# Scores of sixteen later units made in the first seven steps and kept in DRAM; ten early units transposed on TensorE

## The chip, the cores and the metric

The kernel runs on one NeuronCore of a Trainium2 chip. The metric is device time in microseconds (us) for one execution. The kernel before takes 1468.56 us, the median of three runs (1467.57 to 1470.6). One more execution was taken with the hardware profiler; it took 1466.93 us, and its traced span is 1465.2 us.

## What is computed

```python
scores = scale * np.matmul(q, k.transpose(0, 1, 3, 2))       # 8 batches x 8 heads, 576 x 576, head dim 64
kth = np.partition(scores, -32, axis=-1)[..., -32:-31]       # the 32nd largest of each row
scores = np.where(scores >= kth, scores, -1000000000.0)
scores = scores - np.max(scores, axis=-1, keepdims=True)
attn = np.exp(scores)
attn = attn / (np.sum(attn, axis=-1, keepdims=True) + 1e-09)
x = np.matmul(attn, v)                                       # brought to 4608 tokens x 512
h = x @ w_in                                                 # 512 -> 2048
out = np.maximum(0.01 * h, h) @ w_out                        # 2048 -> 512
```

All inputs are float32 except that the weights come as 64-bit words, which the kernel rounds to float32 itself in a prologue.

## The kernel before, in words

**Units and steps.** The attention is cut into 144 units. A unit is 128 query rows of one pair of heads (or twice 64 rows, of the rows left over by 576 = 4 x 128 + 64), so its scores are a tile `s_sb` of 128 partitions x 2 x 576. A batch has 18 units. The main loop (L540) goes over steps s = 0 to 147; four units are in work at once:

- `top_k` of unit s on VectorE (L244): a max and a min of the two halves (L251), then four rounds of MAX8 and MATCH_REPLACE8 (L256, L259). `slot()` puts out one round at a time between the other work of the step.
- `mask` of unit s-1 on GpSimd (L267 to L270), and its exponentials and sums on ScalarE (L273, L278).
- of unit s-2 ("older"): the reciprocals on VectorE (L282), the normalising on ScalarE (L285), then the transposing of the weights into a tile `wT`. The usual way, `transpose` (L287), is by DMA: ScalarE copies the tile in two halves of 16-bit words (`split`, L294), each is written to DRAM (L295), and a transposing DMA reads them back (L299). The other way, `transpose_in_haste` and `keep_transposed` (L301, L312), is nine TensorE transposes into two PSUM tiles and two ScalarE copies (L315). It is used for the units of the tuple `HASTY`, which is (14, 15, 23, 31).
- `scores` (L203): at the end of every even step TensorE makes the scores of units s+2 and s+3 into two "wide" and one "narrow" PSUM tiles (L220), and ScalarE copies them into two `s_sb` tiles (L227), of which there are five.
- `weigh_values` (L329, matmuls L336): the values of two units, at the place that `values_at` (L450) names, and `keep_values` (L350), which copies them on ScalarE into `x`. Normally these copies come late in the step. `at_once` (L562) brings them right after the matmuls, where a chunk of tokens gets complete, and two steps after a unit of `HURRIED` (15, 23, 31).

**The MLP.** When all values of a chunk of tokens (128 for the first two, 256 afterwards) are kept, its MLP becomes ready (`mlp`, L380: first product L360 or L392, activation by ScalarE L365 or L398, second product L404, output copy L413). `mlp_steps` puts out pieces of it between the other operations of each step, as many as a budget allows, which is worked out from the backlog and the step in which the next chunk gets ready (`slot_budget`, L475).

**What sets the order.** The whole block stands under a manual schedule: the order in which the program calls the operations is the order in each engine's queue. [...]So TensorE, ScalarE, GpSimd and VectorE are bound to each other by the sequence of calls within a step, and only the buffers (five `s_sb`, three `wT`, two wide and one narrow PSUM tile, two `ml` tiles for the MLP) let one run ahead of another. All DMAs are issued by SP.

**The start.** Before step 0 the weights are loaded in 16 pieces through three `raw` buffers and rounded on all engines; the first two units' scores are made there (`first_scores`, L229). `load_more` (L489) loads later queries, keys and values; the queries and keys of pairs 5, 6 and 7 of each eight are put into `raw` buffers.

For steps below 20 (`HURRY`), except one and two steps after a hurried unit, the flag `late` puts the reciprocals and normalising of `older` after the second slot of the step.

Of the kernel before, what the change touches and what calls it, by code (L numbers as in the profile page):

```python
# [9 lines left out]
F32 = mybir.dt.float32  # L10
U32 = mybir.dt.uint32
U16 = mybir.dt.uint16
# [8 lines left out]
def kernel(  # L21
# [13 lines left out]
    nc = tc.nc  # L35
    NPAIR, P, S = qT.shape
    D = P // 2
# [9 lines left out]
    HS = S // 2  # L47
# [3 lines left out]
    WCH = 1024  # L51
# [5 lines left out]
    LOADED, LOADED_V = 5, 5  # L57
# [4 lines left out]
    raws = ctx.enter_context(tc.tile_pool(name="raws", bufs=3))  # L62
    work = ctx.enter_context(tc.tile_pool(name="work", bufs=2))
    small = ctx.enter_context(tc.tile_pool(name="small", bufs=5))
    halves = ctx.enter_context(tc.tile_pool(name="halves", bufs=3, space=bass.MemoryType.DRAM))
    ps_sc = ctx.enter_context(tc.tile_pool(name="ps_sc", bufs=1, space=bass.MemoryType.PSUM))
    ps_ml = ctx.enter_context(tc.tile_pool(name="ps_ml", bufs=2, space=bass.MemoryType.PSUM))

# [13 lines left out]
    gT = const.tile([P, NFC, CHMAX], F32, name="gT")  # L82
# [7 lines left out]
    def piece(n):  # L90

        if n < NPIECE // 2:
            j, c = divmod(n, HP)
            return w_in[c][:, j * WCH:(j + 1) * WCH]
        f = 2 * (n - NPIECE // 2)
        return w_out[f // 4][:, f % 4:f % 4 + 2, :].rearrange("p g n -> p (g n)")
# [3 lines left out]
    def load_weights(n):  # L100
        if n >= NPIECE:
            return
        if not AS_WORDS:
            nc.sync.dma_start(piece(n), weights[n])
            return
        raw_of[n] = raws.tile([P, WCH, 4], U16, name="raw")
        flat = raw_of[n].rearrange("p n w -> p (n w)")
        for m, c0, c1 in ROUNDED:
            if m == n:
                nc.sync.dma_start(flat[:, 4 * c0:4 * c1], weights[n][:, 4 * c0:4 * c1])  # L110
# [48 lines left out]
    qk_of, v_of = {}, {}  # L159
# [69 lines left out]
    def first_scores(u):  # L229

        ps = [ps_sc.tile([P, 2, 512], F32, name="wide", bufs=2) for i in range(2)]
        for half in range(2):
            for i, pi, side, r0 in u.parts:
                qt, kt = qk_of[pi]
                d = slice(side * D, (side + 1) * D)
                nc.tensor.matmul(ps[i][:, half, 0:HS], qt[d, u.q0:u.q0 + P],
                                 kt[d, half * HS:(half + 1) * HS], start=True, stop=True)
        yield
        u.both = work.tile([P, 2, S], F32, name="s_sb", bufs=5)
        u.s = [u.both[:, i, :] for i in range(2)]  # L240
        for i in range(2):
            nc.scalar.copy(u.s[i].rearrange("p (h n) -> p h n", h=2), ps[i][:, :, 0:HS])

    def top_k(u):  # L244

# [180 lines left out]
    def mlp_steps(budget):  # L426
        owed[0] += budget
        while owed[0] > 0:
            if running[0] is None:
                if not ready:  # L430
                    owed[0] = 0.0
                    return
                running[0] = mlp(ready.pop(0))
            cost = next(running[0], None)
            if cost is None:
                running[0] = None
            else:
                owed[0] -= cost
                backlog[0] -= cost
# [3 lines left out]
    LAG = 3  # L443
    HURRY = 20
    HURRIED = (15, 23, 31)
    HASTY = (14, 15, 23, 31)
    UNHURRIED = 14
    MIDDLE, END = 0, 1

# [4 lines left out]
        return (n | 1) + LAG - ((n | 1) in HURRIED), END  # L454

    steps = units

    def unit(n):
        return steps[n] if 0 <= n < len(steps) else None

    done_tokens, ready_at = [0] * len(CHUNKS), []
    for n, u in enumerate(steps):
        ch, _ = x_at(u.b * S + u.q0)
# [11 lines left out]
    def slot_budget(s):  # L475

        after = [at for (at, _), _ in ready_at if at >= s]
        until = after[0] if after else s
        if len(after) >= len(CHUNKS) - EARLY:
            return EARLY_SHARE  # L480
        return backlog[0] / ((until + 1 - s) * SLOTS)
# [4 lines left out]
    with tc.manual_schedule():  # L486
        last = {p: n for n, u in enumerate(steps) for p in u.pairs}

        def load_more(s):  # L489

            for of, load, n, lag in ((v_of, load_v, LOADED_V, LAG + 1), (qk_of, load_qk, LOADED + 3, 8)):
                while len(of) < NPAIR and (len(of) < n or last[len(of) - n] + lag <= s):
                    load(len(of))
                    if lag > LAG + 1 and len(of) > n:
                        break


        for n in range(3):
            load_weights(n)
        jobs = [round_weights(*job) for job in ROUNDED] if AS_WORDS else [iter(())] * len(ROUNDED)  # L500
        for n in range(len(jobs) + 1):
            if n == len(jobs) - 1:
                first = first_scores(steps[0])
                next(first, None)
            for job in jobs[max(n - 1, 0):n + 1][::-1]:
                next(job, None)
            if n == len(jobs) - 1:
                next(first, None)
                load_v(0)
                load_v(1)  # L510
            elif n == len(jobs):
                for _ in first_scores(steps[1]):
                    pass
            if n:
                load_weights(n + 2)
            if 0 <= n - len(jobs) + HP + 1 < HP:
                load_qk(n - len(jobs) + HP + 1)

        def weights_of(u):
            reciprocals(u)  # L520
            normalize(u, 0)
            normalize(u, 1)

        def values(*place):
            due = [u for n, u in enumerate(steps) if values_at(n) == place]
            if due:
                po = ps_sc.tile([P, 2, 512], F32, name="wide", bufs=2)[:, 0, 0:2 * P]
                po = po.rearrange("p (u n) -> p u n", u=2)
            else:
                return ()  # L530
            for n, u in enumerate(due):
                weigh_values(u, po[:, n, :])
            return [(u, po[:, n, :]) for n, u in enumerate(due)]

        def keep(weighed, *place):
            for u, po in weighed:
                keep_values(u, po)
            attended(*place)

        for s in range(len(steps) + LAG + 1):  # L540
            cur, old, older, new = unit(s), unit(s - 1), unit(s - 2), ()
            if s % 2 == 0:
                new = [u for u in steps[s + 2:s + 4] if u]
            picks = top_k(cur) if cur else iter(())
            budget = slot_budget(s)

            def slot():
                next(picks, None)

            at_first = s < HURRY and s - 2 in HURRIED  # L550
            if at_first:
                weights_of(older)
            slot()
            if old:
                mask(old, 0)
                mask(old, 1)
            late = s < HURRY and not {s - 1, s - 2} & set(HURRIED)
            if older and not late and not at_first:
                weights_of(older)
            mlp_steps(budget)  # L560
            weighed = values(s, MIDDLE)
            at_once = s - 2 in HURRIED or any(at == (s, MIDDLE) for at, _ in ready_at)  # L562
            if at_once:
                keep(weighed, s, MIDDLE)
            slot()
            if older and late:
                weights_of(older)
            if s - 2 in HASTY:
                transpose_in_haste(older)
            mlp_steps(budget)  # L570
            if old:
                exponents(old, 0)
            mlp_steps(budget)
            if older:
                keep_transposed(older) if s - 2 in HASTY else transpose(older, lambda: mlp_steps(budget))
            if not older or s - 2 in HASTY:
                mlp_steps(budget)
            slot()
            slot()
            mlp_steps(budget)  # L580
            if old:
                exponents(old, 1)
                sums(old)
            mlp_steps(budget)
            if not at_once:
                keep(weighed, s, MIDDLE)
            if new and s < HURRY:
                scores(new)
            keep(values(s, END), s, END)
            if new and s >= HURRY:  # L590
                scores(new)
            budget = slot_budget(s + 1)
            mlp_steps(budget)
            load_more(s)
        mlp_steps(1e9)

# [57 lines left out]
```

## Time and profile before

| what | value |
|---|---|
| median of three runs | 1468.56 us |
| the profiled execution | 1466.93 us, span 1465.2 us |
| TensorE (PE) busy | 1395.2 us, 95% of the span |
| VectorE (DVE) busy | 1320.3 us, 90% |
| ScalarE (ACT) busy | 1100.4 us, 75% |
| GpSimd (POOL) busy | 1097.0 us, 75% |
| DMA | 222.30 MB, 152 GB/s on the mean |
| PE in the chain that ended last | 81% of the span; DVE 16% |
| step 0 begins, VectorE's last instruction ends | 60.9 us, some 1380 us |

A page of the profile gives, for one execution, the busy time of each engine; the span in 40 equal slices, with a digit for the busy share (9 is 90% or more); the granted clock of TensorE in the same slices; groups of instructions by line, as `line engine op out<-in partitions x elements xcount | busy us, mean ns of one | idle before, and what ended it`. A table of stages gives, for a stretch of the span, the busy time (and number of instructions) of each engine, then the granted clock, the DMA share and GB/s. A timeline gives start, length, engine, line, and in square brackets the idle time of that engine before the instruction, and which other one ended it. PEld is TensorE's weight load. One float32 matmul of the program is two MATMUL rows in a trace; a transpose is one.

### The profile page before, as it was taken

To read this page: it belongs to the slowest core of one execution; us is meant where nothing else is said; L and a number is where in the kernel's file an instruction comes from. 1 tells how busy PE (TensorE), PEld (TensorE's weight loads), DVE (VectorE), ACT (ScalarE), POOL (GpSimd) and SP (SyncE) were. 2 spreads that over 40 slices of the span, in tenths; PEclk is the share of its full clock that TensorE was granted. 3 is DMA by queue.
4 is the path that set the end of the run, shared out by engine and by line. 5 is a ranking of instruction groups with operands and counts; after the bars stand their busy time and mean duration, and the time that the engine had idled before them with its cause. 6 is when DMAs were issued, how large, how long until landed. Compare 5 with 4: busy or idle time off the path is not lost.

```text
span 1465.2 us, 24106 instructions
## 1 busy us (share of the span) xinstructions
PE 1395.2 (95%) x8066; PEld 927.8 (63%) x8068; DVE 1320.3 (90%) x3401; ACT 1100.4 (75%) x1984; POOL 1097.0 (75%) x744
## 2 busy tenths in 40 slices
PE   7617999999999999999999999999999999999999
PEld 2314548575757676767676767666666666666674
DVE  7999999999999999999999999999999999999600
ACT  8658878777887777777777777777777777777710
POOL 3388888878888888787878888878788878787700
PEclk9957999999999999999999999999999999999999
DMA  9834534654366455665567545655467555664510
GB/s 329 304 85 133 146 105 116 171 154 136 107 196 185 129 137 155 171 185 137 146 168 193 141 138 132 194 174 148 128 167 202 136 140 144 155 141 132 148 45 14
DMA packets 388940, 222.30 MB, mean 152 GB/s; under 512 B 333904, under 2 KB 333904, under 8 KB 386896
## 3 DMA queue, kind: packets, MB, share of 16 engines
q1 hardware_dynamic: 388816, 220.77, 53.7%
q8 instruction: 63, 1.03, 0.3%
q14 instruction: 61, 0.50, 0.1%
HBM read 46.14 MB, written 92.01 MB: 94 GB/s over the span
## 4 chain that ended last, share of the span: by engine, by line
PE 81%; DVE 16%; ACT 1%; issue 1%; DMA 0%; POOL 0%; DVEq 0%; SPq 0%; ACTq 0%; POOLq 0%
PE pz L404 31%; PE ph L392 30%; PE wide L336 10%; DVE tops L256 6%; PE wide L220 6%; DVE pairs L259 5%; PE narrow L220 3%; DVE pairs L251 2%; DVE w_out L155 1%; DVE scale L152 1%; DVE w_in L155 1%; DMA raw<-in_weights_dram 0%; DVE top L133 0%; DVE scale L131 0%; ACT s_sb L285 0%
## 5 line engine op out<-in xcount | busy, mean ns | idle before, releaser
L269 POOL TENSOR_SCALAR pen<-s_sb,tops 128x576 f32<-128x576 f32 x288 | 637.7, 2214 | 208.7 <-DVE tops L256 144.5
L256 DVE MAX8 tops<-pairs 128x8 f32<-128x288 f32 (+1 forms) x1152 | 635.9, 591 | 0.0
L404 PE MATMUL pz<-w_out,gT 128*128 128x512 f32 x1152 | 505.1, 595 | 2.4 <-ACT scale L365 2.4
L392 PE MATMUL ph<-x,w_in 128*128 128x256 f32 x2176 | 482.9, 381 | 0.9 <-ACT gT L398 0.9
L259 DVE MATCH_REPLACE8 pairs<-tops,pairs 128x288 f32<-128x288 f32 (+1 forms) x864 | 460.2, 538 | 0.0
L392 PEld LDWEIGHTS ph<-x,w_in 128*128 128x128 f32 x2176 | 409.4, 190 | 77.7 <-issue 22.2
L270 POOL TENSOR_TENSOR s_sb<-s_sb,pen 128x576 f32<-128x576 f32 x288 | 406.6, 1412 | 24.0
L404 PEld LDWEIGHTS pz<-w_out,gT 128*128 128x128 f32 x1152 | 216.4, 190 | 267.2 <-issue 262.5
L294 ACT COPY split<-s_sb 128x1152 uint16<-128x1152 uint16 x280 | 309.4, 1146 | 0.0
L285 ACT ACTIVATE s_sb<-s_sb,rz 128x576 f32<-128x576 f32 x288 | 207.6, 773 | 43.4 <-DVE rz L282 43.4
L273 ACT ACTIVATE s_sb<-s_sb,nbias 128x576 f32<-128x576 f32 x288 | 222.3, 772 | 12.8 <-POOL s_sb L270 12.8
L251 DVE TENSOR_TENSOR pairs<-s_sb 128x576 f32<-128x576 f32 x288 | 213.5, 780 | 9.9
L336 PEld LDWEIGHTS wide<-wT,vt 128*64 128x64 f32 x3200 | 161.7, 139 | 65.1 <-issue 34.6
L336 PE MATMUL wide<-wT,vt 128*64 128x128 f32 (+1 forms) x3200 | 179.1, 268 | 22.4 <-ACT s_sb L227 21.1
L398 ACT ACTIVATE gT<-ph 128x512 f32<-128x512 f32 x136 | 80.7, 593 | 56.3 <-PE ph L392 55.6
L227 ACT COPY s_sb<-wide 128x704 f32<-128x704 f32 x142 | 107.2, 755 | 21.0 <-PE wide L220 21.0
L350 ACT COPY x<-wide 128x128 f32<-128x128 f32 (+1 forms) x160 | 32.2, 260 | 112.5 <-PE wide L336 112.4
L220 PE MATMUL wide<-kt,qt 64*128 64x352 f32 (+1 forms) x392 | 76.4, 503 | 26.0 <-ACT s_sb L227 23.0
L413 ACT COPY o_sb<-pz 128x512 f32<-128x512 f32 x36 | 21.1, 586 | 98.0 <-PE pz L404 98.0
L227 ACT COPY s_sb<-narrow 128x448 f32<-128x448 f32 x142 | 68.7, 537 | 1.2 <-PE narrow L220 0.6
L282 DVE RECIPROCAL rz<-ze 128x2 f32<-128x2 f32 x144 | 22.3, 155 | 45.9 <-ACT ze L278 45.8
L259 DVE MATCH_VALUE_LOAD pairs<-tops,pairs 128x8 f32 x864 | 62.6, 72 | 0.0
(61 smaller groups left out, 623.2 us busy)
## 6 DMA issues: line engine op xcount, KB each, us to landing
apart<-split SPq DMA_DIRECT2D x280, 288.0 KB, 2.1
raw<-in_weights_dram SPq DMA_DIRECT2D x15, 1024.0 KB, 6.7
vt<-in_vk_dram SPq DMA_DIRECT2D x32, 320.0 KB, 3.4
out_dram<-o_sb SPq DMA_DIRECT2D x36, 256.0 KB, 2.6
qt<-in_qT_dram SPq DMA_DIRECT2D x20, 288.0 KB, 3.2
kt<-in_kT_dram SPq DMA_DIRECT2D x20, 288.0 KB, 3.7
raw<-in_qT_dram SPq DMA_DIRECT2D x12, 288.0 KB, 3.2
raw<-in_kT_dram SPq DMA_DIRECT2D x12, 288.0 KB, 3.6
```

Of the source, the lines that this page charges most:

```text
L220: nc.tensor.matmul(to[r0:r0 + u.rows, i, :], qt[d, u.q0:u.q0 + u.rows], kt[d, k0:k1], start=True, stop=True)
L251: nc.vector.tensor_tensor(pairs[:, :, n, :], u.both[:, :, 0:HS], u.both[:, :, HS:S], op)
L256: nc.vector.max(out=u.tops[:, i, r, :], in_=rest[i])
L259: nc.vector.match_replace(out=rest[i], in_to_replace=u.tops[:, i, r, :], in_values=rest[i], imm_value=LOWEST)
L269: nc.gpsimd.tensor_scalar(pen, u.s[i], u.tops[:, i, ROUNDS - 1, 7:8], MASKED, ALU.is_lt, ALU.mult)
L270: nc.gpsimd.tensor_tensor(u.s[i], u.s[i], pen, ALU.add)
L273: nc.scalar.activation(u.s[i], u.s[i], AF.Exp, bias=u.nbias[:, i:i + 1], scale=SCALE, accum_out=u.z[:, i:i + 1])
L285: nc.scalar.activation(u.s[i], u.s[i], AF.Copy, bias=0.0, scale=u.rz[:, i:i + 1])
L294: nc.scalar.copy(split, pairs[:, :, h])
L336: nc.tensor.matmul(po[side * D:(side + 1) * D, o, :], vt[:, c, side, :], u.wT[:, c + side * NKC if c + 1 < NKC else c, r:r + n], start=(c ...
L392: nc.tensor.matmul(ph[:, i, 0:n], w_in[c][:, f * P:(f + 1) * P], x[c][:, 0:n], start=(c == 0), stop=(c == HP - 1),)
L404: nc.tensor.matmul(pz[0:m, 0:DMODEL], gT[:, f, r0:r0 + m], w_out[f // 4][:, f % 4, :], start=(f == 0), stop=(f == NFC - 1),)
```

## The change

Three things are changed together.

1. The scores of 16 units, in four sets {24, 25, 32, 33}, {40, 41, 48, 49}, {56, 57, 64, 65} and {72, 73, 80, 81}, are made at the ends of steps 0 to 6 (4, 2, 2, 3, 1, 3 and 1 units). For each set `load_early` loads two keys tiles and four query slices into a `raw` buffer; three sets in the prologue, the fourth when the first has been used. `keep_scores` makes a unit's scores with four matmuls of 288 columns into two PSUM tiles, copies them on ScalarE into one of three slots of `gT` (free until the first MLP), and writes them to a DRAM tile. `fetch_scores` reads them back into an `s_sb` tile, one unit a step, in the step three before that of the unit, after the transposing of `older`. The `scores` calls of steps 22, 30, 38, 46, 54, 62, 70 and 78 fall away.
2. Units 0 to 9 join `HASTY`: they are transposed on TensorE, in steps 2 to 11. And `at_once` now asks for `HASTY` instead of `HURRIED`, so that the values of steps 5 and 9 are copied right after their matmuls too (those of steps 7 and 11 were already).
3. While scores are still to be kept, `load_more` loads the queries and keys of no more than five pairs, so that the `raw` buffers stay free; pairs 5, 6 and 7 follow after step 6.

```diff
+    def load_early(us):
+        raw = raws.tile([P, WCH, 4], U16, name="raw").rearrange("p n w -> p (n w)").bitcast(F32)
+        at = 0
+        for pi in sorted({u.pairs[0] for u in us}):
+            kt = raw[:, at:at + S]
+            nc.sync.dma_start(kt, kT[pi])
+            at += S
+            for u in us:
+                if u.pairs[0] == pi:
+                    early_of[u] = raw[:, at:at + P], kt
+                    nc.sync.dma_start(early_of[u][0], qT[pi][:, u.q0:u.q0 + P])
+                    at += P
+    def keep_scores(u):
+        k = len(kept_of)
+        qt, kt = early_of.pop(u)
+        ps = [ps_sc.tile([P, 2, 512], F32, name="wide", bufs=2) if (2 * k + i) % 3 else
+              ps_sc.tile([P, 2, 512], F32, name="narrow") for i in range(2)]
+        for half in range(2):
+            for i, _, side, _ in u.parts:
+                d = slice(side * D, (side + 1) * D)
+                nc.tensor.matmul(ps[i][:, half, 0:HS], qt[d, :], kt[d, half * HS:(half + 1) * HS],
+                                 start=True, stop=True)
+        both = gT.rearrange("p f n -> p (f n)")[:, k % 3 * 2 * S:(k % 3 + 1) * 2 * S]
+        for i in range(2):
+            nc.scalar.copy(both[:, i * S:(i + 1) * S].rearrange("p (h n) -> p h n", h=2), ps[i][:, :, 0:HS])
+        kept_of[u] = kept.tile([P, 2 * S], F32, name=f"kept{k}")
+        nc.sync.dma_start(kept_of[u], both)
+    def fetch_scores(u):
+        u.both = work.tile([P, 2, S], F32, name="s_sb", bufs=5)
+        u.s = [u.both[:, i, :] for i in range(2)]
+        nc.sync.dma_start(u.both.rearrange("p i n -> p (i n)"), kept_of[u])
...
-    HASTY = (14, 15, 23, 31)
+    HASTY = tuple(range(10)) + (14, 15, 23, 31)
...
+    KEPT = (24, 40, 56, 72)
+    EARLY_SCORES = {0: 4, 1: 2, 2: 2, 3: 3, 4: 1, 5: 3, 6: 1}
...
+        def score_early(count):
+            for _ in range(min(count, len(to_keep))):
+                keep_scores(to_keep.pop(0))
+                if len(to_keep) % 4 == 0 and to_load:
+                    load_early(to_load.pop(0))
...
+                if of is qk_of and to_keep:
+                    while len(of) < LOADED:
+                        load(len(of))
+                    continue
...
+            if n >= len(jobs) - 2:
+                load_early(to_load.pop(0))
...
-            at_once = s - 2 in HURRIED or any(at == (s, MIDDLE) for at, _ in ready_at)
+            at_once = s - 2 in HASTY or any(at == (s, MIDDLE) for at, _ in ready_at)
...
+            if unit(s + 3) in early_units:
+                fetch_scores(unit(s + 3))
...
+            if new and new[0] in early_units:
+                new = ()
             if new and s < HURRY:
                 scores(new)
             keep(values(s, END), s, END)
             if new and s >= HURRY:
                 scores(new)
+            score_early(EARLY_SCORES.get(s, 0))
```

More of the change, by code (lines that the diff above doesn't have):

```diff
@@ L65 @@
     halves = ctx.enter_context(tc.tile_pool(name="halves", bufs=3, space=bass.MemoryType.DRAM))
+    kept = ctx.enter_context(tc.tile_pool(name="kept", bufs=1, space=bass.MemoryType.DRAM))
     ps_sc = ctx.enter_context(tc.tile_pool(name="ps_sc", bufs=1, space=bass.MemoryType.PSUM))
@@ L242, in first_scores @@
             nc.scalar.copy(u.s[i].rearrange("p (h n) -> p h n", h=2), ps[i][:, :, 0:HS])
+    early_of = {}
+    def load_early(us):
[10 more added lines that the diff above has]
+                    at += P
+    kept_of = {}
+    def keep_scores(u):
[17 more added lines that the diff above has]
+        nc.sync.dma_start(u.both.rearrange("p i n -> p (i n)"), kept_of[u])
     def top_k(u):
@@ L487 @@
         last = {p: n for n, u in enumerate(steps) for p in u.pairs}
+        to_keep = [[steps[n] for n in (a, a + 1, a + 8, a + 9)] for a in KEPT]
+        early_units = {u for us in to_keep for u in us}
+        to_load, to_keep = list(to_keep), [u for us in to_keep for u in us]
+        assert all(len(u.pairs) == 1 for u in to_keep)
+        def score_early(count):
[3 more added lines that the diff above has]
+                    load_early(to_load.pop(0))
         def load_more(s):
             for of, load, n, lag in ((v_of, load_v, LOADED_V, LAG + 1), (qk_of, load_qk, LOADED + 3, 8)):
+                if of is qk_of and to_keep:
+                    while len(of) < LOADED:
+                        load(len(of))
+                    continue
                 while len(of) < NPAIR and (len(of) < n or last[len(of) - n] + lag <= s):
@@ L540 @@
         for s in range(len(steps) + LAG + 1):
+            assert s < 7 or not to_keep
             cur, old, older, new = unit(s), unit(s - 1), unit(s - 2), ()
```

## Prediction

> **What bounds the kernel now.** First I read the page's busy shares and its 40 slices, then a table of stages, then what VectorE waits for, then timelines.
>
> ```profile
> PE 1395.2 (95%) x8066; PEld 927.8 (63%) x8068; DVE 1320.3 (90%) x3401; ACT 1100.4 (75%) x1984; POOL 1097.0 (75%) x744
> PE   7617999999999999999999999999999999999999
> DVE  7999999999999999999999999999999999999600
> ```
>
> ```profile
> 60.90:87.30 26.40, 4.56 (x36) 2.89 (x32) 26.16 (x69) 9.59 (x17) 15.69 (x12) 0.69 0.23 85
> 87.30:113.90 26.60, 10.48 (x68) 7.87 (x68) 26.40 (x69) 20.11 (x36) 22.43 (x16) 0.54 0.53 134
> 140.50:167.10 26.60, 26.35 (x161) 15.08 (x161) 26.40 (x69) 22.72 (x44) 22.46 (x16) 1.00 0.49 135
> 386.80:510.90 124.10, 123.06 (x706) 83.96 (x706) 123.14 (x322) 99.49 (x184) 104.76 (x71) 1.00 0.61 170
> 510.90:843.90 333.00, 333.00 (x1996) 229.40 (x1995) 318.23 (x829) 262.27 (x484) 269.52 (x181) 1.00 0.58 158
> ```
>
> The rows' busy times are TensorE, its weight load, VectorE, ScalarE, GpSimd. Steps 0 to 5 (first two rows) are VectorE's: it is full, a step takes 8.8 to 8.87 us by the starts of L251, and TensorE is busy for 15 of 53 us, at about half its clock. From step 9 on TensorE is full too. From 300 us TensorE never rests, and VectorE does: it has 14.8 us idle in the last row. What ends its waits is
>
> ```profile
> DVE rz L282 <- ACT ze L278: 45.8, 45, 7.7
> ```
>
> Reciprocals wait for sums on ScalarE, whose queue stands behind copies of what TensorE is late with. So from step 26 TensorE sets the pace, through ScalarE. Of the 45.8 us, 8.0 come after the last unit; 19.2 lie between 279 and 863 us, where the scores are to be taken away.
>
> ```profile
> 631.90 2.40 PE L336 MATMUL wide<-wT,vt 128*64 128x128 f32 x40
> 634.23 0.86 PE L220 MATMUL wide<-kt,qt 64*128 64x352 f32 x4
> 634.93 0.55 PE L220 MATMUL narrow<-kt,qt 64*128 64x224 f32 x4
> 635.31 0.55 PE L220 MATMUL narrow<-raw 64*128 64x224 f32 x4
> 635.69 0.76 PE L220 MATMUL wide<-raw 64*128 64x352 f32 x4
> 636.38 1.13 PE L392 MATMUL ph<-x,w_in 128*128 128x256 f32 x4
> ```
>
> One `scores` call holds TensorE from 634.23 to 636.38: 2.15 us. Last, places where TensorE did wait, which tell how far ahead it can get:
>
> ```profile
> 186.03 3.70 PE L360 MATMUL ph<-w_in,x 128*128 128x512 f32 x8 [0.86 <-ACT scale L365]
> 192.31 2.42 PE L404 MATMUL pz<-w_out,gT 128*128 128x512 f32 x4 [2.14 <-ACT scale L365]
> 462.85 1.99 PE L392 MATMUL ph<-x,w_in 128*128 128x256 f32 x8 [0.89 <-ACT gT L398]
> ```
>
> **What the Trainium skill says.** "TensorE: Matmul & The Clock Gate", The HAM clock gate: TensorE runs at half clock until it has been busy for a window of about 3.4 us. The trace agrees: 0.54 granted in steps 3 to 5, and the values of step 7 took 4.45 us against 2.40 later. The same page, PE-mode transpose: about 275 ns for one in a kernel. The trace has 283 ns for one, but nine in a row take 1.43 us; I use that. "PSUM — Partial Sum Buffer", Engine vs sequencer instructions: ScalarE, VectorE and GpSimd take their queues strictly first in, first out. The waits above show it. "DMA: Bandwidth & Descriptors", Anatomy of one DMA: about 2 us fixed, most of it the receipt of the write. The 288 KB writes of L295 take 2.1 us to land, so the trace doesn't contradict.
>
> **Scores taken away.** Eight calls x 2.15 us = 17.2 us of TensorE, all after 267 us, and with each the four ScalarE copies of L227 (2.3 us, 448.66 to 450.93), which helps VectorE's waits too. Where does it arrive? Steps 22 and 30: VectorE waits 6.2 us from 279 to 425, more than the 4.3 taken. Steps 46 to 78: five calls, 10.7 us, against 13.0 us of waits from 498 to 863. Step 38: from 386.8 to 510.9 VectorE is full and TensorE is already ahead: at 462.85 it waits for an activation that stands on ScalarE behind a normalising, which waited 2.97 us for VectorE. Getting ahead by another 2.15 only lengthens that wait, so I count this call at nothing. It leaves 7 x 2.15 = **15.1 us**. Next late there is VectorE, at 8.87 us a step: in steps 50 to 86 it keeps some 0.3 us of idle per eight steps.
>
> **Scores made early.** A unit costs 1.24 us of TensorE at full clock (L236, eight rows, 59.91 to 61.15) and 1.18 us of ScalarE (L242, two copies). Sixteen: 19.8 us, up to twice that at half clock, in steps 0 to 6, where TensorE has about 45 us idle: free. ScalarE: in steps 3 to 6 four times normalising 1.44, exponentials 1.76, sums 0.15 and copies of transposes 1.18 (L315), two score calls 2.3 each, eight units 1.18: 32.2 of 35.5 us. That is nearly full, and its waits for TensorE come on top. VectorE needs a step's sums 4.5 us into the next step (L282 at 83.02 in the step of 78.50). If normalising starts N after the step's begin, the sums end at N + 4.4, so nothing is lost while N is under 9.0. I find N = 5 to 7 in steps 2 to 4, 7 to 10 in steps 5 to 7: barely hidden with TensorE warm. Behind the waiting ScalarE stand the score copies and the sums; for them VectorE waits.
>
> **Ten units transposed on TensorE.** ScalarE saves 2.19 (two L294) less 1.18 a unit. TensorE gains 1.43 a unit. Units 0 to 4 fall into its idle time. For units 5 to 9 I walk its queue from the values of step 7 (124.64 before) to the scores of step 12 (174.26), where it was full. Five sets: 7.2 us. In steps 7, 9 and 11 values stand directly ahead of the transposes: TensorE rests while ScalarE copies the values (0.43) and normalises the first half (the transposes of 290.32 begin 0.85 after L285's start); with what lies between that is 1.45 us, three times 4.4. The values of step 7 start some 2 us later, behind the kept scores, but run warm, 2.4 for 4.45: nothing. Sum **+11.5 us** at step 12. In steps 9 and 11 normalising then begins 11 to 12 us after the step's start, so VectorE waits 2 to 3 us for each of the sums. Of the 11.5, the waits at 186.03 and 192.31 (3.0 us) vanish, since TensorE comes later than the activations it waited for. Of the rest about 0.5 us is slack (the scores of 289.6 lie ready 1.9 us before step 26; where VectorE waits it is some 1.4). That leaves **+8.0 us**. Bounds: 0 to 2 if TensorE takes the early work in its idle time and has no round trips; 15 or more if ScalarE is late from step 2 on.
>
> **DMAs and SP.** A kept tile is 590 KB each way. Bounds for a fetch: nothing, or twice the 3.7 us of the 288 KB keys load. I take up to 7.4 us, hidden: it is issued two and a half steps (22 us) ahead of its use. Without that cover each would cost its landing on VectorE. On SP it stands behind a transposing DMA that anyway waits for splits; behind it stand the next splits and outputs. Its buffer is free, the split copies of `older` being done. A delayed `wT` (4.5 us to land) has over one step until its values. The stores hold a `gT` slot for three units, 3.5 us of copies against 2.1 to 4: at worst 1 or 2 us in step 0, where ScalarE rests for most of 20 us. The ten units' split writes and transposes leave SP. The early loads take the place of pairs 5 to 7, which move behind step 6 and are first needed by step 16: nothing.
>
> **Sum.** 15.1 less 8.0 is 7.1 us. On the profiled execution's own time: 1466.93 - 7.1 = 1459.8; the median stands 1.63 above that execution, so **1461.5**.
>
> **Rivals.**
> - *The early work is hidden* (chance 0.15). For it: 45 us of idle and a half clock that denser work would lift; against it: TensorE full from 129 us. Then 15.1 to 17.2 less 0 to 2: 1451.4 to 1455.5.
> - *Nothing measurable* (0.15): TensorE's savings turn into waits for VectorE and ScalarE, since VectorE is within 5% of full everywhere. If only steps 46 to 78 pay (10.7) against 8 to 11.5 early, 1465.9 to 1469.4. For it: the stretch from 387 to 511 us; against: 19.2 us of waits.
> - *Slower* (0.20): ScalarE's queue in steps 2 to 11. Each hasty step now goes normalising, TensorE, copy, sums, at half clock (a set 2.8 us, a kept unit 2.5), and carries kept copies. If each of ten steps makes VectorE wait 2 us, 20 - 15.1 = +4.9: 1473.5. It decides from 1.5 us a step on. For it: ScalarE at 91% by the sum above; against: sums had 3.5 us to spare, and copies shrink by 1 us a unit.
>
> **The numbers.** The forecast has 0.50, its own range 1456 to 1465.5. A measurement tells 0.2% (2.9 us) from no change: faster means under 1465.6, slower over 1471.5. Faster 0.50 + 0.15, same 0.15, slower 0.20. The range 1452 to 1472 takes in the first three cases and leaves out the slower one.
>
> **What would show it.** Right: no L220 calls at the eight steps, and steps 50 to 80 at 8.9 us instead of 9.2; TensorE 2 to 3 us idle near 450; VectorE starting step 26 some 8 us later than 291.5, with waits for L278 in steps 9 to 12. Wrong: step 26 not late (hidden), or VectorE waiting from step 3 on (slower), or fetched units waited for by VectorE.

## The result and the profile after

The changed kernel takes **1489.31 us**, the median of four runs (1486.8 to 1491.1); the kernel before took 1469.53 (1467.57 to 1470.6) beside it. The recorded ratio is 1.0141 (the quotient of these two medians is 1.0135), with a 95% interval of 1.0128 to 1.0154: slower by 1.4%, where 1461.5 had been forecast and 1472 was the range's upper end. The profiled execution took 1489.85 us, its span is 1488.1. Line numbers are now those of the changed kernel: L292 for L251, L323 for L282, L377 for L336, L336 for L295, L340 for L299, L445 for L404; new are L272 and L276 (matmuls and copies of the kept scores), L278 (their store), L283 (the fetch) and L350 (transposes on TensorE).

The page of the changed kernel, its busy shares and the slices of TensorE and VectorE:

```profile
PE 1424.2 (96%) x8158; PEld 945.7 (64%) x8158; DVE 1323.1 (89%) x3401; ACT 1093.0 (73%) x1984; POOL 1098.4 (74%) x744
...
PE   7868999999989999989998999999999999999998
...
DVE  7997899999999999998999899999999999999600
...
PE 82%; DVE 6%; DMA 6%; ACT 5%; issue 1%; SPq 0%; POOL 0%; DVEq 0%; POOLq 0%; ACTq 0%
```

The shares hardly differ, and no engine's digit tells what happened. The last line, the chain that ended last by engine, does: VectorE fell from 16% to 6%, and DMA, which had no share, holds 6% (some 89 us of the span; by lines 3% the transposing DMAs, 1% the split writes, 2% the loads of the weights at the start), ScalarE 5%. The table of stages, for the same stretches of time as before, in which the change stands up to 22 us further back in its work (length, then busy time and instructions of TensorE, its weight load, VectorE, ScalarE and GpSimd, granted clock, DMA share, GB/s):

```profile
60.90:87.30 26.40, 13.86 (x77) 8.67 (x75) 26.19 (x68) 15.90 (x30) 15.56 (x12) 0.80 0.90 308
87.30:113.90 26.60, 21.14 (x92) 13.86 (x92) 25.81 (x69) 19.85 (x40) 22.05 (x15) 0.69 0.28 111
140.50:167.10 26.60, 23.78 (x125) 13.28 (x126) 18.22 (x49) 15.63 (x33) 17.13 (x12) 1.00 0.19 63
386.80:510.90 124.10, 118.17 (x686) 86.18 (x683) 119.05 (x309) 96.13 (x177) 100.33 (x69) 0.97 0.65 175
510.90:843.90 333.00, 323.55 (x1879) 216.35 (x1879) 317.64 (x824) 246.40 (x457) 269.96 (x179) 0.98 0.64 174
```

In steps 0 to 5 VectorE is full as before, while TensorE works two to three times as long as before. From 140 to 167 us everything rests: VectorE is busy for 18.2 us where it had been for 26.4, and TensorE, which was full, rests 2.8 us. In the last two rows TensorE is idle for 5.9 and 9.5 us, where it was for 1.0 and not at all. What ended VectorE's waits, over the span and then from 60 to 220 us, and what ended TensorE's between 279 and 881 us:

```profile
DVE rz L323 <- ACT ze L319: 62.8, 50, 7.7
```

```profile
DVE rz L323 <- ACT ze L319: 16.4, 7, 5.3
```

```profile
PE wide L377 <- DMA wT<-apart: 16.2, 6, 5.9
```

The first line stood at 45.8; the second is its part in the first steps, where the kernel before has 0.2. The third has no counterpart before: TensorE waits for transposed weights.

The sharpest view of all is how late VectorE begins a step against the kernel before (the starts of L292 against those of L251, in the two traces), since it adds up what each step loses or wins. Here for all kernels run:

| kernel | step 26 | step 40 | step 64 | step 84 | step 143 | from 26 to the end |
|---|---|---|---|---|---|---|
| the change | 17.0 | 14.0 | 14.8 | 21.8 | 22.8 | +5.8 |
| e1 no early transposes | 10.0 | 8.8 | 8.1 | 10.1 | 10.4 | +0.4 |
| e2 early transposes only | 7.4 | 6.6 | 6.6 | 6.6 | 7.6 | +0.2 |
| e5 no fetch | 19.7 | 14.3 | 11.1 | 6.6 | 4.6 | -15.1 |
| e6 eight units, free steps | 0.6 | -2.5 | -6.8 | -9.0 | -8.7 | -9.3 |
| e7 eight units, loaded steps | 0.6 | 0.1 | 4.0 | 6.9 | 7.4 | +6.8 |
| e8 as e7, ScalarE's queue | 1.1 | -1.0 | 2.1 | 6.4 | 6.4 | +5.3 |
| e9 all in steps 0 to 2 | 14.2 | 12.9 | 11.8 | 18.0 | 18.1 | +3.9 |
| e10 twelve in steps 0 to 2 | 8.8 | 5.5 | 1.2 | -0.5 | 0.7 | -8.1 |
| e11 twelve, two a step | 4.6 | 2.4 | -1.8 | -3.0 | -6.0 | -10.5 |
| e12 sixteen, two a step | 6.9 | 5.7 | 4.8 | 5.8 | 6.5 | -0.4 |
| e13 copies alone | 1.0 | -1.7 | -1.9 | -0.1 | 2.4 | +1.4 |
| e14 matmuls alone | 2.1 | 0.9 | -0.1 | 0.9 | 1.6 | -0.5 |

The change is 17.0 us late at step 26 and 22.8 at the end, as is TensorE's last matmul (1484.3 us; 1461.5 in the kernel before).

Each row is one execution. Executions of one kernel lie 1.5 to 8.5 us apart (e8's row is 4.4 us faster than the median of its runs, e10's and e11's are 2.3 and 2.4 slower), and step 0 itself begins between 0.1 us early and 2.1 us late. So a difference of one or two us between rows says nothing by itself; the medians of the runs, which stand below, must bear it out.

### The profile page after: what moved, and what is told of

It is laid out like the page before. It is cut to its first block, busy times and chain, and to the rows that moved or that the text cites. A ratio compares the mean times of both kernels' runs of the same rounds, so it can differ in the third digit from the quotient of the medians.

```text
span 1488.1 us, 24395 instructions
## 1 busy us (share of the span) xinstructions
PE 1424.2 (96%) x8158; PEld 945.7 (64%) x8158; DVE 1323.1 (89%) x3401; ACT 1093.0 (73%) x1984; POOL 1098.4 (74%) x744
## 4 chain that ended last, share of the span: by engine, by line
PE 82%; DVE 6%; DMA 6%; ACT 5%; issue 1%; SPq 0%; POOL 0%; DVEq 0%; POOLq 0%; ACTq 0%
PE pz L445 29%; PE ph L433 29%; PE wide L377 10%; PE wide L221 6%; PE narrow L221 3%; DMA wT<-apart 3%; DVE tops L297 2%; DVE pairs L300 2%; PE ph L401 2%; DMA raw<-in_weights_dram 2%; DMA apart<-split 1%; PE wide L350 1%; ACT s_sb L326 1%; ACT split L335 1%; DVE pairs L292 1%
## 5 line engine op out<-in xcount | busy, mean ns | idle before, releaser
L445 PE MATMUL pz<-w_out,gT 128*128 128x512 f32 x1152 | 504.7, 594 | 0.5 <-ACT scale L406 0.5
L445 PEld LDWEIGHTS pz<-w_out,gT 128*128 128x128 f32 x1152 | 216.3, 190 | 263.6 <-issue 261.0
L335 ACT COPY split<-s_sb 128x1152 uint16<-128x1152 uint16 x260 | 287.6, 1147 | 6.9 <-DMA apart<-split 6.8
L292 DVE TENSOR_TENSOR pairs<-s_sb 128x576 f32<-128x576 f32 x288 | 215.8, 788 | 12.9 <-ACT s_sb L228 3.8
L377 PEld LDWEIGHTS wide<-wT,vt 128*64 128x64 f32 x3200 | 159.5, 138 | 61.9 <-issue 36.5
L377 PE MATMUL wide<-wT,vt 128*64 128x128 f32 (+1 forms) x3200 | 178.4, 267 | 19.2 <-DMA wT<-apart 16.5
L391 ACT COPY x<-wide 128x128 f32<-128x128 f32 (+1 forms) x160 | 32.2, 261 | 131.7 <-PE wide L377 131.7
L228 ACT COPY s_sb<-wide 128x704 f32<-128x704 f32 x126 | 95.1, 755 | 24.5 <-PE wide L221 24.5
L323 DVE RECIPROCAL rz<-ze 128x2 f32<-128x2 f32 x144 | 22.8, 158 | 62.8 <-ACT ze L319 62.8
L221 PE MATMUL wide<-kt,qt 64*128 64x352 f32 (+1 forms) x344 | 68.2, 511 | 3.4 <-ACT wT L356 2.7
L300 DVE MATCH_VALUE_LOAD pairs<-tops,pairs 128x8 f32 x864 | 66.8, 77 | 0.0
L228 ACT COPY s_sb<-narrow 128x448 f32<-128x448 f32 x126 | 60.9, 536 | 4.7 <-PE narrow L221 4.1
```

The source lines that it names most:

```text
L221: nc.tensor.matmul(to[r0:r0 + u.rows, i, :], qt[d, u.q0:u.q0 + u.rows], kt[d, k0:k1], start=True, stop=True)
L292: nc.vector.tensor_tensor(pairs[:, :, n, :], u.both[:, :, 0:HS], u.both[:, :, HS:S], op)
L300: nc.vector.match_replace(out=rest[i], in_to_replace=u.tops[:, i, r, :], in_values=rest[i], imm_value=LOWEST)
L335: nc.scalar.copy(split, pairs[:, :, h])
L377: nc.tensor.matmul(po[side * D:(side + 1) * D, o, :], vt[:, c, side, :], u.wT[:, c + side * NKC if c + 1 < NKC else c, r:r + n], start=(c ...
L445: nc.tensor.matmul(pz[0:m, 0:DMODEL], gT[:, f, r0:r0 + m], w_out[f // 4][:, f % 4, :], start=(f == 0), stop=(f == NFC - 1),)
```

## The experiments

The theory after the result: besides the transposes, which cost about what I had forecast, two things that I had counted at nothing make the change slow. Ahead of step 26 it is waits between ScalarE and TensorE, which each early unit adds; behind it, the fetch makes the writes of the split weights land late, so that TensorE waits for `wT`. The rivals: ScalarE's or TensorE's busy time alone; SP's queue in place of the DMA engines; and savings that never were.

**e1 and e2: one half each.** e1 is the changed kernel without the early transposes, as the diff has it; e2 is the kernel before with these two lines changed the other way.

```diff
-    HASTY = tuple(range(10)) + (14, 15, 23, 31)
+    HASTY = (14, 15, 23, 31)
-            at_once = s - 2 in HASTY or any(at == (s, MIDDLE) for at, _ in ready_at)
+            at_once = s - 2 in HURRIED or any(at == (s, MIDDLE) for at, _ in ready_at)
```

> The changed kernel with units 0 to 9 transposed by DMA again and their values copied where they were copied before; the 16 units' scores are still made early, kept and fetched. Theory: most of the 17 us by which step 16 is late come from the round trips between ScalarE and TensorE in the hasty steps, so step 26 should be late by at most 4 us instead of 17.0; the lateness of the steps in which a fetch meets other loads (37/38, 61/62, 77/78) stays. Time about 1476 (1473 to 1479). Rival (the kept scores alone hold up ScalarE): step 26 late by 10 us or more, time 1483 or more.

> The kernel before with only units 0 to 9 transposed on TensorE, and the values of steps 5 and 9 copied right after their matmuls; no scores are kept. Theory: the round trips alone, without the kept copies in ScalarE's queue, make step 26 late by 8 to 11 us, which then stays to the end: about 1478 (1475 to 1481). Rival (round trips are hidden, it is the kept copies that crowd ScalarE): step 26 late by under 3 us, time 1468 to 1472.

e1: 1478.28 us, ratio 1.0078 (1.0063 to 1.0093). e2: 1474.94, 1.0054 (1.0039 to 1.0069). By step 26 e2 is 7.4 us late and e1 10.0; together 17.4, for 17.0 in the change. So the price ahead of step 26 is the sum of two, and the transposes cost about what was forecast (8.0). The theory of e1 fell: it gave the kept scores 4 us at most, and its range of time was met only because e1 loses less than the change behind step 26 (0.4 us for 5.8). For e2 the 7.4 lies just under the 8 to 11 expected.

**e5: no fetch.** The fetched tiles are filled by a copy on ScalarE.

```diff
-        nc.sync.dma_start(u.both.rearrange("p i n -> p (i n)"), kept_of[u])
+        nc.scalar.copy(u.both, cur.both)
```

> The changed kernel without the fetch from DRAM: ScalarE copies the scores of the unit then at work into the tile instead, so the 16 units are worked on with other units' scores (their own are still made and written to DRAM, but not used). TensorE's saving and the early phase are as in the changed kernel. Theory: step 26 is late by 17 us as before; the jumps at 37/38, 61/62 and 77/78 (13.4 us) vanish; end 17 less 8 to 15 us: 1472 to 1479. Rival (the fetches are innocent, TensorE gets ahead of the transposed weights whatever is fetched): the jumps stay, 1486 to 1490.

1470.3 us, 1.0025 (1.0014 to 1.0036). From step 26 to the end it wins 15.1 us, where the change loses 5.8, although ScalarE makes 16 copies more. The fetch costs the change **20.9 us**, and the saving on TensorE is there in full. The time lies 1.7 us below the range that was expected. TensorE's wait for `wT`, 16.2 us in the change, is this in e5, in a stretch from 279 to 900 us:

```profile
PE wide L377 <- DMA wT<-apart: 1.4, 3, 0.9
```

**Where the fetch strikes.** The change's TensorE at the second fetch for units 40 and 41, then SP's queue there:

```profile
439.61 1.31 PE L377 MATMUL wide<-wT,vt 128*64 128x128 f32 x20
446.86 2.40 PE L377 MATMUL wide<-wT,vt 128*64 128x128 f32 x20 [5.93 <-DMA wT<-apart]
```

```profile
434.46 0.57 SPq L283 DMA_DIRECT2D s_sb<-kept  x1
435.08 0.42 SPq L175 DMA_DIRECT2D vt<-in_vk_dram  x1
435.60 0.85 SPq L336 DMA_DIRECT2D apart<-split  x2
442.04 2.69 SPq L340 DMA_TRANSPOSE wT<-apart  x1
```

And SP's queue in the kernel before:

```profile
417.63 0.53 SPq L174 DMA_DIRECT2D vt<-in_vk_dram  x1
421.51 1.38 SPq L295 DMA_DIRECT2D apart<-split  x2
424.71 2.29 SPq L299 DMA_TRANSPOSE wT<-apart  x1
```

The transposing DMA waits until both split halves have landed. In the kernel before, it is issued 1.8 us after the second write's issue ends (421.51 + 1.38 to 424.71). In the change the writes stand just behind a fetch and a load of values, and it takes 5.6 us (436.45 to 442.04). TensorE resumes 4.8 us after that issue. This is unit 37; of a pair of units the second is always the one in a hurry. In the kernel before, the weights of units 21, 29, 45, 53, 61 and 69 lie ready only 2.9 to 3.3 us ahead of use (issue of the transposing DMA and its 4.6 us, against the unit's first L336 matmul), those of 77 2.6, those of 37 not at all; even units have 8 to 14 us.

**e6, e7 and e8: where and on which queue.** Eight units in four sets of two, without early transposes; the early scores stand 4, 2, 2 in steps 0 to 2. In e6 the fetches stand in steps that load nothing, in e7 in steps that load values or queries and keys, in e8 as in e7 but issued by ScalarE.

```diff
-    KEPT = (24, 40, 56, 72)
-    EARLY_SCORES = {0: 4, 1: 2, 2: 2, 3: 3, 4: 1, 5: 3, 6: 1}
+    KEPT = ((32, 33), (48, 49), (56, 57), (72, 73))       # e6
+    KEPT = ((24, 25), (40, 41), (64, 65), (80, 81))       # e7, e8
+    EARLY_SCORES = {0: 4, 1: 2, 2: 2}
...
-        nc.sync.dma_start(u.both.rearrange("p i n -> p (i n)"), kept_of[u])      # e8
+        nc.scalar.dma_start(u.both.rearrange("p i n -> p (i n)"), kept_of[u])
```

> Only eight units' scores are kept (32, 33, 48, 49, 56, 57, 72, 73: those whose fetches fall into steps without loads of queries, keys or values), made in steps 0 to 2; units 0 to 9 transposed by DMA. Theory: early lateness under 2 us, no jump at a fetch, four score calls saved at 1.3 to 2.15 us each: 1462 to 1466. Rival (a fetch costs what it saves wherever it stands, or the transposed weights, 1 to 3 us ahead of their use, leave nothing to win): 1468 to 1472.

> As e6 with the other eight units (24, 25, 40, 41, 64, 65, 80, 81), whose fetches fall into steps 21/22, 37/38, 61/62 and 77/78, in which keys and queries or values are loaded too. Same number of kept scores, same early steps. Theory (a fetch together with other loads holds up the split writes, so the transposed weights of an odd unit come late): four calls saved, 8.6 us, less jumps of 10 to 14 us: step 88 late by 2 to 6 us, time 1470 to 1474. Rival (the place of the fetch doesn't matter): as e6, step 88 early by 9 us, 1459.

> As e7, with the fetches issued by ScalarE's DMA queue instead of SP's. Theory in two forms. If the split writes stand in line behind the fetch in SP's queue, they pass it now, the jumps shrink to less than half, and the time is 1461 to 1466. If it is the bytes that the same 16 DMA engines must move, it stays within 3 us of e7.

e6: **1459.03 us**, 0.9952 (0.9935 to 0.9968), faster than both kernels, and 3 us better than its range: from step 26 it wins 9.3 us, for 8.6 us of TensorE's time taken away. e7: 1475.77, 1.0058 (1.0038 to 1.0077), 1.8 us over its range, and 6.9 us late at step 88 where 2 to 6 had been expected. e8: 1477.7, 1.006 (1.0036 to 1.0083), within 3 us of e7 as the second form said, though its runs lie 8.1 us apart. Between e6 and e7 the work is equal and so is the start (0.6 us late at step 26), and 16.1 us lie between them at the end. TensorE's waits for `wT` from 279 to 900 us, of e6, e7 and e8 in turn:

```profile
PE wide L377 <- DMA wT<-apart: 0.2, 1, 0.2
```

```profile
PE wide L377 <- DMA wT<-apart: 11.8, 4, 6.2
```

```profile
PE wide L377 <- DMA wT<-apart: 11.7, 7, 4.0
```

Moving the fetch off SP's queue doesn't help; it moves the delay. From the second write's issue to that of the transposing DMA, units 21, 37, 61 and 77 take 5.5 to 6.0 us in e7 and 3.0 to 4.2 in e8; but 35, 59 and 75 take 4.2 to 5.2 in e8, for 2.2 to 2.7 in e7, and TensorE now waits for these three too. ScalarE issues the fetches earlier than SP came to them, those of units 40 and 41 by 6 and 10 us. SP's queue of e8 at unit 35, whose writes have no fetch ahead of them there:

```profile
403.19 1.92 SPq L336 DMA_DIRECT2D apart<-split  x2
409.43 2.48 SPq L340 DMA_TRANSPOSE wT<-apart  x1
```

ScalarE issued a fetch at 404.25, in the same moment as SP the second write; that write took 5.1 us to land, 2.1 being the median in the kernel before. So a fetch needn't stand in SP's queue to delay the writes. What e8 leaves in place is the other part of that line: SP stands at a transposing DMA until the writes have landed, and issues the loads and writes behind it late. The Trainium skill, "DMA: Bandwidth & Descriptors", Issuing engines are not separate DMA queues, says that DMAs of every issuing engine run on the same 16 DMA engines and interleave there; the 11.7 us of e8 beside 11.8 and the write of unit 35 agree. A fetch delays the writes in e6 too; SP's queue of e6 at the second fetch of {32, 33}:

```profile
345.97 0.53 SPq L283 DMA_DIRECT2D s_sb<-kept  x1
346.55 1.33 SPq L336 DMA_DIRECT2D apart<-split  x2
353.09 2.31 SPq L340 DMA_TRANSPOSE wT<-apart  x1
```

Here it took 5.2 us after the issues' end (347.88 to 353.09), and 5.5 us counted from the second write's own issue; by that count it is 2.2 us (the median of the kernel before), and 2.7 to 4.0 at the other three sets. The 3 us by which units 29, 45, 53 and 69 are ahead just cover it: TensorE waits for none of the four, and e6's 0.2 us are at unit 37. Where loads come on top, in e7, it is 5.5 to 6.2 us each time, more than the 3 us can cover. The loads alone do no such harm: they stand in the kernel before too, where units 21, 37, 61 and 77 take 2.2 to 2.8 us, and units 20, 36, 60 and 76, which have 8 us and more to spare, at most 5.1.

**e9 and e10: the early scores in fewer steps.** e9 is e1 with all sixteen in steps 0 to 2, e10 is e6 with two more sets and all in steps 0 to 2.

```diff
-    EARLY_SCORES = {0: 4, 1: 2, 2: 2, 3: 3, 4: 1, 5: 3, 6: 1}
+    EARLY_SCORES = {0: 6, 1: 5, 2: 5}                                       # e9
-    KEPT = ((32, 33), (48, 49), (56, 57), (72, 73))
-    EARLY_SCORES = {0: 4, 1: 2, 2: 2}
+    KEPT = ((32, 33), (48, 49), (56, 57), (72, 73), (84, 85), (92, 93))     # e10
+    EARLY_SCORES = {0: 4, 1: 4, 2: 4}
```

> As e1 (16 units kept and fetched, no early transposes), but the early scores made 6, 5 and 5 at the ends of steps 0, 1 and 2 instead of over steps 0 to 6. Theory (the kept copies cost only where ScalarE also splits, normalises and keeps values, from step 3 on): step 26 late by under 3 us instead of 10.0, the later part as e1: 1469 to 1473. Rival (16 kept scores cost ten us wherever they stand): 1476 to 1480.

> As e6 with four more units (84, 85, 92, 93; fetches in steps 81/82 and 89/90, where nothing else is loaded), twelve in all, made 4, 4 and 4 in steps 0 to 2. Theory: two more calls saved at 2.1 us, early lateness up to 2 us: 1453.5 to 1457.5. Rival (VectorE's waits are used up, or the early steps crowd again): 1459 or more.

e9: 1485.14 us, 1.011 (1.0092 to 1.0128), worse than e1 and outside both expectations: the theory, that only steps from 3 on are crowded, fell, and so did the rival's constant price. e10: 1465.58, 0.9986 (0.9979 to 0.9994), a miss by 8 us: 8.8 us late by step 5, and the sets {84, 85} and {92, 93} won nothing in its trace. A likely reason is that the weights of units 81 and 89, whose split writes stand just behind the second fetch of each, lie ready only 1.1 us ahead in the kernel before; TensorE waits 2.4 us for those of 81. Part of the burst's price is a third wait. ScalarE in e10, at the last unit of step 1:

```profile
87.54 0.64 ACT L276 COPY gT<-wide 128x576 f32<-128x576 f32 x1 [3.69 <-DMA kept<-gT]
```

Its slot of `gT` was still being stored: that store, issued at 79.33 us behind five loads of values, queries and keys, landed at 87.44.

**e11 and e12: never more than two units a step after step 0.**

```diff
+    KEPT = ((32, 33), (48, 49), (56, 57), (72, 73), (104, 105), (120, 121))     # e11, on e6
+    EARLY_SCORES = {0: 6, 1: 2, 2: 2, 3: 2}
+    EARLY_SCORES = {0: 6, 1: 2, 2: 2, 3: 2, 4: 1, 5: 2, 6: 1}                   # e12, on e1
```

> Six sets are kept: the four of e6 and {104,105} and {120,121}, so that the two new fetches stand in steps 101, 102, 117 and 118, which load nothing, ahead of the splits of units 101 and 117, whose transposed weights land about 3 us before they are used. The early scores are spread 6, 2, 2, 2 over steps 0 to 3, never more than two a step once step 0 is over. Theory (the early price comes from a burst of copies within one step, the fetch's price from bytes that meet loads ahead of a tight unit): step 26 late by 1.5 us or less, two more calls saved at 2.15 us, 1453.5 to 1457.5 us. Rival (each kept unit has its price wherever it stands, or the later steps have nothing more to win): step 26 late by 4 us or more, or no gain at the new sets, 1459 us or more.

> The kernel of e1 (sixteen units kept, no early transposes on TensorE) with the early scores spread 6, 2, 2, 2, 1, 2, 1 over steps 0 to 6 in place of 4, 2, 2, 3, 1, 3, 1: two more in step 0 and one less in each of steps 3 and 5; sets and fetches stay. Theory (the third unit of a step is what runs over): step 26 late by 4 us or less in place of 10.0, the later steps as in e1, 1469 to 1473 us. Rival (the number of kept units counts, however they are spread): step 26 late by 8 us or more, 1476 to 1480 us.

e11: 1458.8 us, 0.995 (0.9938 to 0.9963). It falls 1.3 us short of its window: 4.6 us late by step 26 (2.1 of it at step 0 already), which is the rival's sign, and the two late sets win 2.9 us (step 84 to the end) in place of 4.3, which is not. It equals e6. e12: 1473.46, 1.0039 (1.0025 to 1.0052), between the two expectations, so undecided: 6.9 us late for 10.0. Spreading helps by a third; 4.0 us of the rest come between steps 8 and 9, behind the units kept in steps 5 and 6 (e1 loses 4.1 there).

**e13 and e14: which engine.** e1 with one half of the early work. e13 copies keys from SBUF in place of scores, with no matmul; e14 makes the matmuls, and nothing reads them.

```diff
-                nc.tensor.matmul(ps[i][:, half, 0:HS], qt[d, :], kt[d, half * HS:(half + 1) * HS],      # e13
-                                 start=True, stop=True)                                         # e13
-            nc.scalar.copy(both[:, i * S:(i + 1) * S].rearrange("p (h n) -> p h n", h=2), ps[i][:, :, 0:HS])
+            nc.scalar.copy(both[:, i * S:(i + 1) * S], kt)                          # e13
+            nc.sync.dma_start(kept_of[u][:, i * S:(i + 1) * S], kt)                 # e14, matmuls stay
-        nc.sync.dma_start(kept_of[u], both)                                         # e14
```

> The kernel of e1 with the matmuls of the kept scores left out: ScalarE makes its two copies of 128x576 a unit from the keys tile in SBUF, so the sixteen units are worked with copies of keys in place of their scores. Theory (the early price of 10.0 us is the round trip between ScalarE and TensorE, not the busy time of either): without a TensorE to wait for, the copies fit as the prediction counted them, step 26 late by 3 us or less, 1468 to 1471.5 us. Rival (ScalarE's own time is what runs over): step 26 late by 7 us or more, 1475 us or more.

> The kernel of e1 with the copies of the kept scores left out: TensorE makes all scores, nobody reads them, and the keys tile is stored in DRAM twice a unit in their place, so the sixteen units are worked with copies of keys. Theory (the round trip is the price): TensorE's work alone lies in its idle time except ahead of the values of steps 5 and 7, so step 26 is late by 1 to 4 us, 1469 to 1473 us. Rival (TensorE's own time ahead of the values and of the first MLP is the price): step 26 late by 7 us or more, 1475 us or more.

e13: 1467.96 us, 1.0009 (0.9999 to 1.0019). e14: 1470.02, 1.0027 (1.0015 to 1.0039). At step 26 they are late by **1.0 and 2.1 us; together the same work costs 10.0** (the medians stand 1.4, 3.4 and 10.7 us above those of the kernel before beside them). Neither engine's time is the price, nor is it the later loading of pairs 5 to 7, which both have too: some 7 us come only where copies and matmuls wait for each other. ScalarE at the end of step 3, three units, in e1 and then in e13 (whose lines stand seven higher):

```profile
102.06 1.16 ACT L276 COPY gT<-wide 128x576 f32<-128x576 f32 x2
104.11 0.64 ACT L276 COPY gT<-narrow 128x576 f32<-128x576 f32 x1 [0.89 <-PE narrow L272]
105.06 0.64 ACT L276 COPY gT<-wide 128x576 f32<-128x576 f32 x1 [0.30 <-PE wide L272]
...
107.62 1.44 ACT L326 ACTIVATE s_sb<-s_sb,rz 128x576 f32<-128x576 f32 x2
```

```profile
98.41 3.52 ACT L269 COPY gT<-raw 128x576 f32<-128x576 f32 x6
101.84 1.44 ACT L319 ACTIVATE s_sb<-s_sb,rz 128x576 f32<-128x576 f32 x2
```

The three units hold ScalarE for 5.56 us in e1 (102.06 to 107.62) and 3.43 in e13. In e1 each copy after the first two waits for its matmuls, 0.3 to 0.9 us, and these could only start when a PSUM tile had been copied out (one waited 4.97 us for L276); behind it all stand normalising, exponentials and the sums for which VectorE waits.

## Why the prediction was wrong, by its own steps

- **Scores taken away**, 15.1 us: right, though the match to the tenth is luck, for e5's runs lie 4.2 us apart. e5 wins 15.1, by parts 5.3 for steps 22 and 30 (I had 4.3), nothing from step 36 to 48, so the call of step 38 indeed pays nothing, and 9.7 for steps 46 to 78 (10.7).
- **Ten units transposed on TensorE**, +8.0 us: right in size, with 7.4 in e2, and in kind. In e2 VectorE loses 5.6 us in steps 8 to 10 and 2.2 in steps 13 and 14; I had put the waits into steps 9 to 12. That the change loses time from step 5 on is not the transposes' doing: at step 9 it is 10.1 us late, e1 9.7 and e2 0.4, and at step 12 15.1, 10.0 and 5.5. ScalarE and TensorE of e2 in step 9 (lines of the kernel before):

```profile
156.22 0.60 ACT L365 ACTIVATE scale<-ph 128x512 f32<-128x512 f32 x1 [1.82 <-PE ph L360]
```

```profile
153.03 1.43 PE L309 MATMUL wide<-ident,s_sb 128*128 128x128 f32 x9 [1.21 <-ACT s_sb L285]
```

  Normalising begins 11.3 us into the step (forecast 11 to 12). TensorE rests 1.21 us for the first normalised half, transposes, then takes up the MLP, and the activation that waits for the MLP holds up ScalarE for 1.82 us, with exponentials and sums behind it; VectorE waits 3.7 us for the sums.
- **Scores made early**, "free" and "barely hidden with TensorE warm": the first failed step, 10.0 us in e1. I added busy times, ScalarE's 32.2 of 35.5 us and TensorE's idle 45, and asked whether each fits. Both do (1.0 and 2.1 us). What I left out is that a copy and the matmuls before it alternate on three PSUM tiles, with TensorE at partial clock (0.69 in steps 3 to 5 of the change): a unit kept ScalarE for 1.85 us in step 3 of e1, not 1.18, and normalising began 10.5 us into the next step, over the 9.0 that I had myself set as the bound. I had written that "its waits for TensorE come on top" and put no number there. The values of step 7, which I let start some 2 us later and counted at nothing, are the largest single piece, 4.1 us of e1's 10.0:

```profile
134.41 0.84 PE L272 MATMUL narrow<-raw 64*128 64x288 f32 x1 [5.02 <-ACT s_sb L228]
136.63 2.86 PE L377 MATMUL wide<-wT,vt 128*64 128x128 f32 x40
```

  In TensorE's queue they stand behind the matmuls of step 6's kept unit, which waited 5.02 us until ScalarE had copied the scores out of a PSUM tile. They begin 9.0 us into the step, 1.9 in the kernel before. The eight units of e6 in steps 0 to 2 are nearly free indeed, 0.6 us.
- **DMAs and SP**, counted at nothing: the second failed step, and the greater, 20.9 us. The fetch itself is hidden as I said: VectorE waits for no fetched tile. But that a delayed `wT` "has over one step until its values" was assumed, not read. For the odd unit of a pair the trace of the kernel before holds 3 us, not a step of 8.9. I asked what the fetch waits for and who waits for the fetch, and not who else has bytes in the DMA engines just behind it.
- **Sum.** 15.1 won, 17.0 lost ahead of step 26 and 20.9 after it make +22.8; 7.1 won had been forecast. The rival *Slower* had the right place for the first loss (20 us guessed, 17.0 found), but the nearness is in part luck: it spread the 20 over ten steps, and its sign, VectorE waiting from step 3 on, did not come (the first wait, of 0.6 us, is in step 5). No rival had the second loss. Of the signs named for being right, TensorE idle near 450 us came, but from a late `wT` and with 5.9 us; steps 50 to 80 came down from 9.26 us a step to 9.22 only, and to 9.00 in e5.

How the 20.9 us spread over single fetches, and why the same sets cost only 14.6 to 16.5 us in e1, e12, e13 and e14 (15.1 and the table's last column), is not settled. TensorE's waits for `wT` show a part: 16.2 us in the change, 11.5 to 12.6 in the four, with most of the difference at units 61 and 77. That the bytes in the DMA engines cause the delay, and not the traffic in DRAM, was only argued: no run tells these apart. Nor does one tell how much is the delayed writes and how much is SP, which stands until they have landed.

## What to carry to other kernels

When a transfer is added, list the transfers that are issued just behind it, and read from the trace by how many us each lands ahead of its use: the smallest of these, not the new transfer's own cover, is the budget. When work is moved into idle time of two engines that hand tiles to each other, busy times that fit aren't enough: price the hand-over, unit by unit, and count what stands behind it in the queue. Eight units, made 4, 2 and 2 in steps 0 to 2 and fetched in steps without loads, keep 0.5% of gain (1459.03 us); sixteen lose 0.4% (e12) to 0.8% (e1), and 1.4% with the transposes.

## What the runs showed of the hardware

- Two 288 KB writes to DRAM, from the second's issue to that of the DMA that waits for them, take 2.2 us at the median, between 2.7 and 5.5 us with one 576 KB load ahead of them (e6), and 5.5 to 6.2 with a load of values or of queries and keys beside it (e7). With the 576 KB load issued by ScalarE the writes near it took 3.0 to 8.5 us (e8).
- The six copies of three units from PSUM took 5.56 us in hand-over with TensorE (e1), and six copies of the same shape from SBUF 3.52 us in a row (e13).
- The store of a kept tile took 2.8 us to land in the change (median), 3.6 in e1, 3.5 in e10 and 4.4 in e11; the longest, in e9, took 8.6 us.
